# The sixth product of gate ahead of the fifth of value, and the last gate between two scalings

## The chip, the core and the metric

The kernel runs on one core of one Trainium2 chip. The metric is the device time of one execution in microseconds; the runs of the kernel before have a median of 323.09 us (five runs, 322.84 to 324.94). The engines are called as the profile calls them: PE (matrix products; PEld is its weight load), DVE (VectorE), ACT (ScalarE), POOL (GpSimd) and SP, which issues DMAs.

## The reference

Two stages, one after the other. Linear attention without a softmax, with an RMS norm, over 8 batches, 8 heads, 576 tokens and 64 channels a head:

```python
kv = np.einsum('bhsd,bhse->bhde', k, v)
out = np.einsum('bhsd,bhde->bhse', q, kv)
rms = np.sqrt(np.mean(out * out, axis=-1, keepdims=True) + 1e-06)
x = (out / rms * g_norm).transpose(0, 2, 1, 3).reshape(4608, 512)
```

Then a gated feed-forward layer on the 4608 tokens, with 512 channels and 1536 hidden ones:

```python
g, val = x @ w_gate, x @ w_val
ffn_out = gelu(g) * val @ w_out
out = x + sigmoid(x @ w_res) * ffn_out
```

## The kernel before

**Blocks.** The feed-forward layer runs in nine blocks of 512 tokens: block b holds the first 512 tokens of batch b, and block 8 the remaining 64 of all eight. While PE works on block m, the attention of batch m + 2 is done beside it, and its output becomes the input of a later block.

**Seven products.** Most of the layer's products are made by a scheme of seven block products in place of eight: quadrants of tokens and of weights are added beforehand (`ts` are the token sums, `wsg`, `wsv` and `wo_ts` weight sums, `hid_s` sums of the hidden layer), and the partial results are shared through copies and additions.

**A group of gate and value.** `gv_group` (L916) makes four of the twelve slices of the hidden layer, for gate (`g`) and value (`v`) side by side. A string in `ORDERS` (L911) is the order in which every engine is given its work. A word such as `5v` is product 5 of value: four matmuls on PE, each of 128x256. `Eg` and `Ev` are copies on ACT that seed a second PSUM bank with product 1; `dg` and `dv` are copies on ACT that keep product 5; `F` and `c` words are additions on DVE (the sum of bank A and the kept copy); `g11` to `g22` are gelus on ACT; `h11` to `h22` are gelu times value, on DVE except `h22`, which is on POOL. Product 1 opens bank A, 5 opens bank F, 6, 7 and 4 add to bank A, 2 adds to bank E and 3 to bank F. So 6 has to wait until the copy `E` has read bank A, 7 until the addition `F` has read it, and 4 until the addition `c` has. The last group of a block has the order `True`, the others `False`; a dictionary `amid` hangs further work of the attention behind a word.

Blocks 2 to 6 are called whole (`whole`, L1384): all three of their groups are made like this. Block 7 has the groups too, in another sequence.

**The end of a block.** `others` (L709) makes five of the seven products of w_out, each of twelve matmuls, with the gates `pf` (DVE: sigmoid branch times ffn output) between them. The last product, in bank `A`, is followed by the gate of quarter (1, 1) on POOL and the gate of quarter (1, 0) on DVE. `aside(...)` at the names `F`, `00`, `22`, `01`, `11` and `end` is where other work is put in.

**What hangs there.** `plan_attn_ahead` (L1388) puts the norm of batch m + 2 behind `F` and the scalings `a_t` (L334: attention output times inverse norm, one DVE instruction of 128x512 each, four per batch) at the border between blocks. Scalings 0 and 1 go to `11`, ahead of the block's last product (for block 1 the first goes to `01` and the second to `11`); scaling 2 follows the word `1v` of the next block's first group and scaling 3 follows `Fv`, with a DMA transpose behind it. A scaling reads the attention's product from PSUM and so frees its bank.

**Banks.** `banks_of` (L1478) hands the banks on. In the first group of a whole block after another, bank A of gate is the old `D`, A of value the old `E`, E of gate the old `F`, and E of value the old `A`, which the block's last gate, `pf((1, 0), w["A"])`, reads. The banks of `5g` and `5v` are those of the attention's outputs 0 and 1, which scalings 0 and 1 free. So at each border `Ev` waits for the last gate, `5g` for scaling 0 and `5v` for scaling 1.

Each engine takes its instructions in the order in which the program gives them; there is no scheduler behind it.

Of the kernel before, what the change touches and what calls it, by code (L numbers as in the profile page):

```python
# [18 lines left out]
def kernel(  # L19
# [876 lines left out]
    def token_sums(blk, eng):  # L896
# [12 lines left out]
        ]  # L909

    ORDERS = {  # L911
        False: "1g 1v Eg 5g Ev 5v dg 6g dv 6v Fg 2g Fv 2v 7g g11 7v cg 3g cv 3v h11 g12 4g g21 h12 4v g22 h21 h22",
        True: "1g 1v Eg 5g Ev 5v dg 6g dv 6v Fg 2g Fv 2v 7g g11 7v cg 3g cv 3v h11 g22 4g g12 h12 4v g21 h22 h21",
    }

    def gv_group(blk, g, banks, amid, last):  # L916

        if blk not in hids:
            hids[blk] = hidp.tile([P, NF, NJ * P], FP16, tag="hid", name="hid")
        f0 = GF * g  # L920
        ps, ge, sb = {}, {}, {}

        def tile_of(n, u):
            ps[n, u] = pmoe.tile([P, 2, PR], FP32, name=n + u, bank=banks[u, n])
            return ps[n, u]

        def product(p, u):
            ws = wg_c if u == "g" else wv_c
            n = {1: "A", 2: "E", 3: "F", 4: "A", 5: "F", 6: "A", 7: "A"}[p]
            first = p in (1, 5)  # L930
            out_ = tile_of(n, u) if first else ps[n, u]
            s_of = {3: 3, 5: 0, 6: 1, 7: 2}
            t_of = {4: 3, 5: 0, 6: 1, 7: 2}
            quad = {1: (0, 0), 2: (0, 1), 4: (1, 1)}
            xq = {1: (0, 0), 2: (1, 0), 3: (1, 1)}
            for r in range(2):
                for c in range(2):
                    if p in s_of:
                        lhsT = gv_sums[u, g][:, s_of[p], r, c, :]
                    else:  # L940
                        i, k = quad[p]
                        parts = w_quadrant(ws, f0, i, k)
                        lhsT = parts[0][:, r, c, :] if len(parts) == 1 else parts[r][:, 0, c, :]
                    rhs = x_sums[blk][:, t_of[p], :, c, :] if p in t_of else x_quadrant(blk, *xq[p])[:, :, c, :]
                    nc.tensor.matmul(  # L945
                        out_[:, r, :],
                        lhsT=lhsT,
                        rhs=rhs,
                        start=(first and r == 0 and c == 0),
                        stop=(c == 1),  # L950
                        skip_group_check=True,
                    )

        def seed(u):
            nc.scalar.copy(out=tile_of("E", u), in_=ps["A", u])  # L955

        def keep(u):
            sb["d", u] = attnp.tile([P, 2, PR], FP32, tag="sq", bufs=3, name="d")
            nc.scalar.copy(out=sb["d", u], in_=ps["F", u])  # L959

        def plus(u, n):
            if n == "F":
                dst = tile_of("F", u)
            else:
                dst = sb["c", u] = attnp.tile([P, 2, PR], FP32, tag="o32", bufs=3, name="c")
            nc.vector.tensor_tensor(out=dst, in0=ps["A", u], in1=sb["d", u], op=ALU.add)  # L966

        quarter = {"11": ("E", 0, 0), "12": ("F", 0, 1), "21": ("A", 1, 0), "22": ("c", 1, 1)}

        def source(q, u):  # L970
            n = quarter[q][0]
            return sb[n, u] if n == "c" else ps[n, u]

        def gelu(q):
            ge[q] = moep.tile([P, 2, PR], FP16, tag="ge", name="ge")
            nc.scalar.activation(out=ge[q], in_=source(q, "g"), func=AF.Gelu)  # L976

        def hidden(q):
            _, i, j = quarter[q]
            dst = hids[blk][:, f0 + i : f0 + GF : 2, j * PR : (j + 1) * PR]  # L980
            eng = nc.gpsimd if q == "22" else nc.vector
            eng.tensor_tensor(out=dst, in0=ge[q], in1=source(q, "v"), op=ALU.mult)  # L982

        for word in ORDERS[last].split():
            if word[0].isdigit():
                product(int(word[0]), word[1])
            elif word[0] == "E":
                seed(word[1])
            elif word[0] == "d":
                keep(word[1])  # L990
            elif word[0] in "Fc":
                plus(word[1], word[0])
            elif word[0] == "g":
                gelu(word[1:])
            else:
                hidden(word[1:])
            for f in amid.get(word, ()):
                f()
# [120 lines left out]
    first = {}  # L1119
# [219 lines left out]
    amid_out = {}  # L1339
# [15 lines left out]
    def aside_out(blk, ahead_of, *fs):  # L1355
        amid_out.setdefault(blk, {}).setdefault(ahead_of, []).extend(fs)
# [20 lines left out]
    WHOLE = 2  # L1377
    GROUPS = {blk: (1, 2) for blk in range(2, WHOLE)} | {blk: (0, 1, 2) for blk in range(WHOLE, B - 1)} | {B - 1: (1, 0, 2), B: (0, 1, 2)}
    amid_gv = {}
# [4 lines left out]
    def whole(blk):  # L1384

        return WHOLE <= blk < B - 1

    def plan_attn_ahead(b):  # L1388

        rem = pair(b) is not None  # L1390
        m = b - 2
        assert rem == (m in GROUPS)
        act, pool = nc.scalar.copy, nc.gpsimd
        begin = [lambda: attn_begin(b), lambda: d_qT(b)]
        if rem:
            at_word(m, 0, "h22", begin.pop(0), lambda: d_rem_qT(b))
        if m in GROUPS:
            for i in range(2):
                half = lambda i=i: by_token(b, act, slice(2 * i, 2 * i + 2))
                if whole(m):  # L1400
                    at_word(m, i, "g11", half)
                else:
                    at(m, 2 + i, half)
            if whole(m):
                at_word(m, 1, "g11", *begin)
            else:
                at(m, 3, *begin)
            if b + 1 < B:
                at(m, 2 * GF, lambda: load_behind(b))
            last = len(GROUPS[m]) - 1  # L1410
        else:
            at(m, 8, lambda: by_token(b, act, slice(0, 2)))
            at(m, 9, lambda: by_token(b, act, slice(2, 4)), *begin)
            at(m, NF - 1, lambda: a_kv(b, act))
            at(m, NF, lambda: load_behind(b))
        if rem:
            at_word(m + 2, 0, "cv", lambda: a_g(b, NJ, NJ + 1))
            own = 2 * pair(b) + 1 == b
            at_word(m, last, "5v" if own else "3g", lambda: a_rem_kv(b))
            at_word(m, last, "dv" if own else "g12", lambda: kv_out(b))  # L1420
            if own:
                at_word(m, last, "3g", lambda: rem_mm(b))
            at_word(m, last, "g12", lambda: rem_out(b))
        else:
            at(m, NF, lambda: a_o(b), lambda: a_ss(b, 0), lambda: a_ss(b, 1))
            aside_out(m, "D", lambda: a_ss(b, 2), lambda: a_ss(b, 3))
        aside_out(m, "F", lambda: a_norm(b, 0, NJ + rem, pool))
        first = [lambda: new_block(b), lambda: a_t(b, 0), lambda: a_t(b, 1)]
        if m + 1 == WHOLE:
            aside_out(m, "01", *first[0:2])  # L1430
            aside_out(m, "11", first[2])
        elif whole(m + 1):
            aside_out(m, "11", *first)
        else:
            at(m, NF + 3, *first)
        if whole(m + 1):
            t = [lambda j=j: a_t(b, j) for j in range(NJ)]
            if rem:
                at_word(m + 1, 0, "h21", lambda: a_t(b, NJ), lambda: d_xT(b, NJ, NJ + 1))
            for i, word, fs in (  # L1440
                (0, "1v", t[2:3]),
                (0, "Fv", [t[3], lambda: d_xT(b, 0, NJ)]),
                (1, "cv", [lambda: a_g(b, 0, 2)]),
                (2, "Fv", [lambda: a_g(b, 2, NJ)]),
            ):
                at_word(m + 1, i, word, *fs)
            return
        for j in range(2, NJ + rem):
            at(m + 1, j - 2, lambda j=j: a_t(b, j))
        at(m + 1, 1, lambda: d_xT(b, 0, NJ))  # L1450
        at_word(m + 1, 1, "Fv", lambda: a_g(b, 0, 2))
        at_word(m + 1, 1, "cv", lambda: a_g(b, 2, NJ))
# [64 lines left out]
    for blk in range(B + 1):  # L1517
# [21 lines left out]
        else:  # L1539
            slots = [lambda f=f: m_gval(blk, f) for f in range(NF)]  # L1540
            groups = GROUPS.get(blk, ())
            if groups:
# [6 lines left out]
                def group(i, blk=blk, ends=ends):  # L1549
                    if i == 0:  # L1550
                        ends.extend(banks_of(blk))
                        if blk + 2 < B:
                            o = att_at[blk]
                            pattn.opening = o[2:] + o
                    gv_group(blk, GROUPS[blk][i], ends[i], amid_gv.get((blk, i), {}), i == len(GROUPS[blk]) - 1)

                for i in range(len(groups)):
                    slots[n + GF * i] = lambda i=i: group(i)
# [77 lines left out]
```

## Time and profile before

| | |
|---|---|
| median of five runs | 323.09 us (322.84 to 324.94) |
| the profiled execution | 323.7 us, its span 321.9 us |
| mean granted PE clock | 0.996 |
| ACT, idle before `Eg` until PE's bank A | 27.8 us, 8 times |
| DVE, idle before `Fg` until ACT's `d` | 10.0 us, 12 times |
| ACT, idle before `Ev` until PE's bank F | 3.6 us, 5 times |
| DVE scaling `t<-op,ny` | 28 of them, 677 / 682 / 693 ns (lowest, median, highest) |
| DVE gate `osb<-th,wA` | 7 of them, 675 / 677 / 678 ns |
| ACT copy `Ev` | 22 of them, 554 / 570 / 578 ns |

The profile is of one execution. A row of a timeline has the start, the duration, the engine, the line, the operation with its output and inputs, and in brackets how long the engine stood idle before it and which instruction released it. Rows of one engine can overlap, since the next instruction starts before the last has fully ended; the end of a PE row is modelled. Where a wait is for several things, the profile names the one that came last by its own reckoning.

First groups of whole blocks begin at 91.94 us (block 2), 125.20 (3), 158.07 (4), 190.95 (5) and 224.06 (6); block 7 begins at 255.14.

### The profile page before, as it was taken

To read this page: it belongs to the slowest core of one execution; us is meant where nothing else is said; L and a number is where in the kernel's file an instruction comes from. 1 tells how busy PE (TensorE), PEld (TensorE's weight loads), DVE (VectorE), ACT (ScalarE), POOL (GpSimd) and SP (SyncE) were. 2 spreads that over 40 slices of the span, in tenths; PEclk is the share of its full clock that TensorE was granted. 3 is DMA by queue.
4 is the path that set the end of the run, shared out by engine and by line. 5 is a ranking of instruction groups with operands and counts; after the bars stand their busy time and mean duration, and the time that the engine had idled before them with its cause. 6 is when DMAs were issued, how large, how long until landed. Compare 5 with 4: busy or idle time off the path is not lost.

```text
span 321.9 us, 7756 instructions
## 1 busy us (share of the span) xinstructions
PE 312.3 (97%) x3044; PEld 246.9 (77%) x3044; DVE 273.7 (85%) x486; ACT 210.0 (65%) x385; POOL 187.3 (58%) x249
## 2 busy tenths in 40 slices
PE   8999999999999999999999999999999999999993
PEld 3545755444788888888888888888888888888882
DVE  6788879799888899989998999799989677897774
ACT  3773685465838794878487848785767466736770
POOL 2792350573869379757875777516761375396332
PEclk9999999999999999999999999999999999999998
DMA  8999999799994899479947893800340003000204
GB/s 249 327 202 202 195 205 186 168 160 171 170 110 83 196 137 96 81 214 126 105 78 219 107 125 67 227 6 0 68 147 2 0 3 133 0 2 36 97 2 130
DMA packets 76694, 38.90 MB, mean 121 GB/s; under 512 B 42098, under 2 KB 74354, under 8 KB 76658
## 3 DMA queue, kind: packets, MB, share of 16 engines
q0 software_dynamic: 38752, 17.17, 42.1%
q1 hardware_dynamic: 37328, 20.71, 25.2%
q10 hardware_dynamic: 578, 0.52, 0.5%
q8 instruction: 24, 0.39, 0.5%
q14 instruction: 12, 0.10, 0.1%
HBM read 38.80 MB, written 9.44 MB: 150 GB/s over the span
## 4 chain that ended last, share of the span: by engine, by line
PE 83%; DMA 11%; ACT 1%; SPq 1%; DVE 1%; issue 1%; POOL 0%; DVEq 0%; ACTq 0%
PE Av L945 12%; PE wA L515 11%; PE Ag L945 11%; PE Fv L945 6%; PE Fg L945 6%; DMA wo<-in_moe_w_out_dram 5%; PE rA L566 4%; PE gps L410 3%; PE fps L447 3%; PE vps L410 3%; PE wE L515 3%; PE wF L515 3%; PE Ev L945 3%; PE Eg L945 3%; PE wD L515 3%; DMA wg<-in_moe_w_gate_dram 3%
## 5 line engine op out<-in xcount | busy, mean ns | idle before, releaser
L982 POOL TENSOR_TENSOR hid<-ge,c 128x512 f16<-128x512 f16 x22 | 25.6, 1163 | 40.7 <-ACT ge L976 40.7
L515 PEld LDWEIGHTS <-hid_s 128*128 128x128 f16 x384 | 37.6, 98 | 4.5 <-issue 0.2
L945 PEld LDWEIGHTS <-wsv 128*128 128x128 f16 x352 | 33.9, 97 | 7.1 <-issue 2.2
L945 PEld LDWEIGHTS <-wsg 128*128 128x128 f16 x352 | 34.3, 98 | 4.0
L361 POOL TENSOR_TENSOR t<-t,g 128x512 f16<-128x512 f16 x32 | 37.1, 1188 | 0.0
L702 POOL TENSOR_TENSOR osb<-osb,t 128x512 f32<-128x512 f32 x28 | 34.1, 1247 | 0.0
L955 ACT COPY Eg<-Ag 128x512 f32<-128x512 f32 x22 | 12.8, 582 | 27.8 <-PE Ag L945 27.8
L515 PEld LDWEIGHTS <-hid 128*128 128x128 f16 x288 | 28.2, 98 | 3.5
L945 PEld LDWEIGHTS <-wg 128*128 128x128 f16 x264 | 25.8, 98 | 3.2
L945 PEld LDWEIGHTS <-wv 128*128 128x128 f16 x264 | 25.8, 98 | 3.2
L966 DVE TENSOR_TENSOR Fg<-Ag,d 128x512 f32<-128x512 f32 x22 | 15.3, 697 | 14.8 <-ACT d L959 10.0
L945 PE MATMUL Av<-ts,wsv 128*128 128x256 f16 x176 | 26.4, 272 | 1.2 <-ACT Ev L955 1.1
L945 PE MATMUL Ag<-ts,wsg 128*128 128x256 f16 x176 | 26.4, 273 | 0.0
L258 DVE TENSOR_REDUCE ss<-sq 128x8 f32<-128x512 f32 x32 | 20.5, 679 | 2.4 <-ACT sq L253 2.4
L398 ACT ACTIVATE ge<-gps 128x512 f16<-128x512 f32 x20 | 11.7, 597 | 14.3 <-PE gps L410 14.1
L515 PE MATMUL wA<-wo_ts,hid_s 128*128 128x256 f16 x168 | 20.6, 272 | 0.0
L976 ACT ACTIVATE ge<-Eg 128x512 f16<-128x512 f32 x22 | 13.1, 597 | 9.7 <-PE Eg L945 9.7
L976 ACT ACTIVATE ge<-c 128x512 f16<-128x512 f32 x22 | 13.7, 625 | 7.8 <-DVE c L966 7.8
L345 DVE TENSOR_TENSOR t<-op,ny 128x512 f16<-128x512 f32 x28 | 18.4, 683 | 0.5 <-POOL ny L319 0.4
L976 ACT ACTIVATE ge<-Fg 128x512 f16<-128x512 f32 x22 | 13.0, 591 | 8.8 <-PE Fg L945 6.5
L966 DVE TENSOR_TENSOR c<-Ag,d 128x512 f32<-128x512 f32 x22 | 15.1, 688 | 4.2 <-PE Ag L945 4.2
L410 PE MATMUL gps<-xT,wg 128*128 128x512 f16 x72 | 18.5, 379 | 0.0
(219 smaller groups left out, 857.8 us busy)
## 6 DMA issues: line engine op xcount, KB each, us to landing
out_dram<-osb SPq DMA_DIRECT2D x14, 512.0 KB, 3.6
qraw<-in_q_dram POOLq DMA_DIRECT2D x7, 512.0 KB, 6.6
k<-in_k_dram POOLq DMA_DIRECT2D x7, 512.0 KB, 8.5
v<-in_v_dram POOLq DMA_DIRECT2D x7, 512.0 KB, 10.6
wg<-in_moe_w_gate_dram POOLq DMA_DIRECT2D x2, 512.0 KB, 8.4
wv<-in_moe_w_val_dram POOLq DMA_DIRECT2D x2, 512.0 KB, 9.0
wo<-in_moe_w_out_dram POOLq DMA_DIRECT2D x2, 512.0 KB, 14.5
out_dram<-osb SPq DMA_DIRECT2D x4, 256.0 KB, 4.5
```

What stands on the lines that cost most here:

```text
L258: nc.vector.tensor_reduce(out=out_, in_=sqs.pop((b, i)), op=ALU.add, axis=mybir.AxisListType.X)
L345: nc.vector.tensor_tensor(out=t, in0=o, in1=scale, op=ALU.mult)
L361: eng.tensor_tensor(out=t_t[blk][:, jj, :], in0=t_t[blk][:, jj, :], in1=g16, op=ALU.mult)
L410: nc.tensor.matmul(ps[:, j0 * P : j1 * P], lhsT=w[:, cc, :], rhs=xT_t[blk][:, j0:j1, cc, :], start=(cc == 0 and j0 == 0), stop=(cc == NP - ...
L515: nc.tensor.matmul(ps[:, e - es[0], :], lhsT=a[:, f, e * P : (e + 1) * P], rhs=b[:, f, :], start=(start and e == es[0] and f == 0), stop=( ...
L566: nc.tensor.matmul(out_[:, e, :], lhsT=x_[:, e, cc, :], rhs=w_[:, cc, :], start=(first and e == 0 and cc == 0), stop=(cc == 1), skip_group ...
L702: nc.gpsimd.tensor_tensor(out=res_all[of], in0=res_all[of], in1=t_t[blk][of], op=ALU.add)
L945: nc.tensor.matmul(out_[:, r, :], lhsT=lhsT, rhs=rhs, start=(first and r == 0 and c == 0), stop=(c == 1), skip_group_check=True,)
L955: nc.scalar.copy(out=tile_of("E", u), in_=ps["A", u])
L966: nc.vector.tensor_tensor(out=dst, in0=ps["A", u], in1=sb["d", u], op=ALU.add)
L976: nc.scalar.activation(out=ge[q], in_=source(q, "g"), func=AF.Gelu)
L982: eng.tensor_tensor(out=dst, in0=ge[q], in1=source(q, "v"), op=ALU.mult)
```

## The change

A third order, `None`, is used for the first group of the whole blocks 2 to 6. It reads `5g 6g Ev 5v dg 6v dv` where `False` reads `5g Ev 5v dg 6g dv 6v`. On PE this puts the four matmuls of `6g` ahead of those of `5v`; ACT's order stays `Eg`, `Ev`, `dg`, `dv`.

At the border ahead of these blocks, scaling 1 moves from `11` (ahead of the last product and the last gate) to the front of `end` (behind the last gate). On DVE the order becomes scaling 0, gate (1, 0), scaling 1, scaling 2 in place of scaling 0, scaling 1, gate, scaling 2. In block 1 two token sums stood at `end`, and scaling 1 goes ahead of them.

```diff
     ORDERS = {
+        None: "1g 1v Eg 5g 6g Ev 5v dg 6v dv Fg 2g Fv 2v 7g g11 7v cg 3g cv 3v h11 g12 4g g21 h12 4v g22 h21 h22",
         False: "1g 1v Eg 5g Ev 5v dg 6g dv 6v Fg 2g Fv 2v 7g g11 7v cg 3g cv 3v h11 g12 4g g21 h12 4v g22 h21 h22",
...
-    def gv_group(blk, g, banks, amid, last):
+    def gv_group(blk, g, banks, amid, order):
...
-        for word in ORDERS[last].split():
+        for word in ORDERS[order].split():
...
         first = [lambda: new_block(b), lambda: a_t(b, 0), lambda: a_t(b, 1)]
-        if m + 1 == WHOLE:
-            aside_out(m, "01", *first[0:2])
-            aside_out(m, "11", first[2])
-        elif whole(m + 1):
-            aside_out(m, "11", *first)
+        if whole(m + 1):
+            aside_out(m, "01" if m + 1 == WHOLE else "11", *first[0:2])
+            amid_out[m].setdefault("end", []).insert(0, first[2])
...
-                    gv_group(blk, GROUPS[blk][i], ends[i], amid_gv.get((blk, i), {}), i == len(GROUPS[blk]) - 1)
+                    order = None if i == 0 and whole(blk) else i == len(GROUPS[blk]) - 1
+                    gv_group(blk, GROUPS[blk][i], ends[i], amid_gv.get((blk, i), {}), order)
```

## The prediction

> **What bounds the kernel now.** I read the page's busy line first, then PE's rows in the list of waits, then the timelines of PE, VectorE (DVE) and ScalarE (ACT) around the start of a block.
>
> ```profile
> PE 312.3 (97%) x3044; PEld 246.9 (77%) x3044; DVE 273.7 (85%) x486; ACT 210.0 (65%) x385; POOL 187.3 (58%) x249
> ```
>
> PE is the bound: 9.6 us of the span are left beside its busy time, more than half of them in the first and last of the page's forty slices. So the change can only win what PE stands still for. The list of PE's waits has one row after 60 us:
>
> ```profile
> PE Av L945 <- ACT Ev L955: 1.1, 5, 0.2
> ```
>
> The timeline puts the five at 107.17 (third group of block 2, outside the change) and at 127.78, 160.66, 193.53 and 226.63: the sixth product of value ("6v") in the first group of blocks 3 to 6. Block 3 on PE, a row per product of four matmuls:
>
> ```profile
> 125.20 0.60 PE L945 MATMUL Ag<-xT,wg 128*128 128x256 f16 x4
> 125.64 0.60 PE L945 MATMUL Av<-xT,wv 128*128 128x256 f16 x4
> 126.07 0.60 PE L945 MATMUL Fg<-ts,wsg 128*128 128x256 f16 x4
> 126.53 0.60 PE L945 MATMUL Fv<-ts,wsv 128*128 128x256 f16 x4
> 126.97 0.60 PE L945 MATMUL Ag<-ts,wsg 128*128 128x256 f16 x4
> 127.78 0.60 PE L945 MATMUL Av<-ts,wsv 128*128 128x256 f16 x4 [0.22 <-ACT Ev L955]
> ...
> 129.09 0.60 PE L945 MATMUL Ag<-ts,wsg 128*128 128x256 f16 x4
> 129.62 0.60 PE L945 MATMUL Av<-ts,wsv 128*128 128x256 f16 x4
> ...
> 131.40 0.60 PE L945 MATMUL Av<-ts,wv 128*128 128x256 f16 x4
> ```
>
> These are 1g, 1v, 5g, 5v, 6g, 6v, then 7g, 7v and 4v, the last of the group's fourteen. Undisturbed products start 0.437 us apart (the second group of block 2: 13 steps in 99.31 to 104.99). So the cost is larger than the 0.22 shown, since a row ends 0.16 after the next can start: 6v is 0.37 late, 7v 0.09, 5v 0.02, 4v 0.03. From 1g to 4v that is 131.40 - 125.20 - 13 x 0.437 = 0.52 us per block. Now the two engines that feed it:
>
> ```profile
> 124.55 0.67 DVE L698 TENSOR_TENSOR osb<-th,wF 128x512 f32<-128x512 f32 x1
> 125.19 1.29 DVE L345 TENSOR_TENSOR t<-op,ny 128x512 f16<-128x512 f32 x2
> 126.40 0.68 DVE L698 TENSOR_TENSOR osb<-th,wA 128x512 f32<-128x512 f32 x1
> 126.99 0.68 DVE L345 TENSOR_TENSOR t<-op,ny 128x512 f16<-128x512 f32 x1
> 128.27 0.70 DVE L966 TENSOR_TENSOR Fg<-Ag,d 128x512 f32<-128x512 f32 x1 [0.59 <-ACT d L959]
> 128.88 0.69 DVE L966 TENSOR_TENSOR Fv<-Av,d 128x512 f32<-128x512 f32 x1
> ```
>
> ```profile
> 125.84 0.57 ACT L955 COPY Eg<-Ag 128x512 f32<-128x512 f32 x1 [3.54 <-PE Ag L945]
> 127.16 0.57 ACT L955 COPY Ev<-Av 128x512 f32<-128x512 f32 x1 [0.75 <-PE Fv L945]
> 127.64 0.59 ACT L959 COPY d<-Fg 128x512 f32<-128x512 f32 x1
> 128.12 0.60 ACT L959 COPY d<-Fv 128x512 f32<-128x512 f32 x1
> ```
>
> The copy Ev goes into the bank that the last gate (osb<-th,wA) reads; the gate ends at 127.08 and Ev starts at 127.16. The profile names PE's Fv (5v) as releaser, because that ends at 126.53 + 0.60 = 127.13. Block 2 tells the two apart:
>
> ```profile
> 93.76 0.57 ACT L955 COPY Ev<-Av 128x512 f32<-128x512 f32 x1 [0.62 <-DVE osb L698]
> ```
>
> Its gate ends at 93.68, while its 5v, started at 93.25, ends only at 93.85: Ev starts before 5v is over, so it waits for the gate. Latencies read from these rows: DVE to PE 0.05, DVE to ACT 0.08, ACT to PE 0.05, PE to ACT 0.04, ACT to DVE 0.04; a DVE row starts 0.60 after the one before.
>
> **The change, part by part.** No instruction is added or removed; in the built program only PE and DVE change order, and ACT, POOL and SP issue the same lists, so no DMA moves in its queue (the transpose behind the fourth scaling comes with it, 0.46 earlier).
>
> *The gate goes ahead of the second scaling* (blocks 2 to 6). In block 3 the first scaling keeps 125.19, the gate takes 125.79 to 126.47, the second scaling 126.40 to 127.08, and the third stays at 126.99. The gate also waits for the last product of w_out (ends 125.36); queued behind it would be the scalings, but it is ready 0.4 us ahead of its new place, so this wait costs nothing. Ev can start at 126.55 instead of 127.16 and ends at 127.12.
>
> *5v waits for the second scaling*, which frees its bank: from 127.08 + 0.05 = 127.13 on, 0.6 later than now. Left in its place (126.51) it would stall 0.62.
>
> *6g goes ahead of 5v* and fills that hole. It waits for the copy Eg (ends 126.41, so 126.46) and PE reaches it at 126.51: no stall; it could slip to 126.69 before it pushed 5v. PE is free for 5v at 126.95; 5v starts at 127.13: **a new stall of 0.18**. Then 6v at 127.57 (Ev done at 127.17), against 127.78.
>
> *Downstream.* d(Fg) runs 127.03 to 127.62, so Fg starts at 127.66 (0.61 earlier). d(Fv) waits for 5v (127.73) and runs 127.77 to 128.37; Fv 128.41 to 129.10 (0.47 earlier). 7g is due at 128.88 and Fg ended at 128.35; 7v is due at 129.32, Fv allows 129.15: the 0.09 stall goes. 4g is due at 130.63 and its sum c ends at 130.29; 4v at 131.06, with its c ended at 130.89. So 4v starts at 131.06 against 131.40: **0.34 us per block**. What is late next is DVE in the second group: there Fv ends at 135.66 and 7v starts at 135.76, hardly any room. But DVE runs without a pause from Fv of the first group up to there and is itself 0.46 earlier, more than PE's 0.34.
>
> Blocks 4, 5 and 6 have the same rows (4v at 164.27, 197.15, 230.25 against 163.94, 196.80, 229.91 by the same steps): 0.33, 0.35, 0.34.
>
> *Block 2 gives nothing.* There DVE has two token sums behind the gate and no pause from 91.80 on, and both orders hold the same instructions:
>
> ```profile
> 94.87 0.70 DVE L966 TENSOR_TENSOR Fg<-Ag,d 128x512 f32<-128x512 f32 x1
> ```
>
> Fg has no idle before it. 6v moves from 94.39 to 94.17, but Fv still starts at 95.48 and holds 7v at 96.22.
>
> *One rule against the row.* The Trainium skill, "VectorE: DVE Perf Modes", section "The DRAIN you can't avoid", says that after a VectorE operation the next starts only once the pipeline has emptied (and allows that some start earlier). Taken strictly, with 0.68 a step from the end of osb<-th,wF at 125.22, the second scaling would end at 127.26, 5v start at 127.31, and a block win 0.16: 0.6 in all. The rows start 0.60 apart while lasting 0.68, here and in each of the blocks, so I take 0.60.
>
> *Buffers.* In the built program one gelu of block 2's second group now waits for POOL, and one of its third no longer; block 3 has it the other way round. The gelu starts at 104.81, and the POOL row it needs ended at 100.52: nothing either way.
>
> Sum: 0 + 0.34 + 0.33 + 0.35 + 0.34 = **1.36 us**. Behind the stage PE is without other waits to the end but the one at 107.17, which lies ahead. The profiled execution took 323.7 us (span 321.9): it would take 322.3. It stands 0.6 above the median of the runs shown, 323.09, so against that I forecast **321.7 us**, 0.42% faster.
>
> **The rivals.**
> - *Hidden anyway.* DVE proves to be the limit in blocks 3 to 6 too, as it is in block 2, and hands the time back in the second group: 0 to 0.6 won (the strict rule above is inside), about 322.9. For it: DVE at 85%, the 0.05 to 0.1 of room before 7v. Against: 0.59 idle before each Fg.
> - *More than reckoned.* 5v isn't held by the second scaling and all gaps close: 4 x 0.52 plus block 2's 98.01 - 91.94 - 13 x 0.437 = 0.39, together 2.5: 320.6. Partly so, without 5v's 0.18: 2.1, 321.0. Against: DVE has no pause that would bring the scaling forward.
> - *Slower.* Ev does wait for 5v, as the profile's row says. Then 5v at 127.13 puts Ev at 127.77 to 128.34, 6v at 128.39 and, by way of d and Fv, 7v at 130.23: 0.61 later than now, in each of five blocks 3.0: 326.1. It decides as soon as Ev starts later than 127.16. Against it stands block 2's row, where Ev started with 5v still running.
>
> **How the numbers follow.** A difference of 0.5%, 1.6 us, is about what a measurement of this kernel can tell from no change. The forecast has 0.70, hidden 0.12, more 0.13, slower 0.05. The forecast's own spread (321.2 to 322.3: steps read to 0.02 us twenty times over, and medians that move by 0.3) has about a quarter beyond 321.5, so faster gets 0.16 + 0.13 = 0.29, slower 0.05, and 0.66 stays within. The range runs from 320.7, near all gaps closed, to 323.2, nothing won.
>
> **What would show it.** In the new trace: in blocks 3 to 6 the stall sits at 5v with about 0.18 between starts beyond 0.437, DVE named as its cause, and none at 6v; Ev starts 0.6 earlier relative to 1g; Fg's idle before it is gone or tiny; 1g to 4v takes 5.86 instead of 6.20, while block 2 keeps 6.07. I am wrong if 6g stalls on Eg, if 7v is still late in blocks 3 to 6, or if PE waits anew in the second group.

## The result, and the profile after

The changed kernel has a median of 321.94 us (321.27 to 329.68, 31 runs; the highest is a disturbed execution and is left out of the ratio) against 323.04 us before (52 runs): ratio 0.9955, interval 0.9945 to 0.9966. By the ratio 1.45 us (1.10 to 1.78) are won, 1.10 by the medians; 1.36 were forecast.

Its profiled execution has a span of 320.2 us, 1.7 shorter than the one before. Of that, 0.38 us lies ahead of block 2 (its first product starts at 91.56 against 91.94), where the change has not begun; that is scatter between executions (the one before waited 0.62 us for a DMA at 43.34, the one after did not). From there to the first product of block 7 it is 161.81 us against 163.20: 1.39 us.

PE in the first group of block 3, the same rows as before (start, duration, engine, line, operation):

```profile
124.79 0.60 PE L946 MATMUL Ag<-xT,wg 128*128 128x256 f16 x4
125.23 0.60 PE L946 MATMUL Av<-xT,wv 128*128 128x256 f16 x4
125.66 0.60 PE L946 MATMUL Fg<-ts,wsg 128*128 128x256 f16 x4
126.10 0.60 PE L946 MATMUL Ag<-ts,wsg 128*128 128x256 f16 x4
126.72 0.60 PE L946 MATMUL Fv<-ts,wsv 128*128 128x256 f16 x4
127.15 0.60 PE L946 MATMUL Av<-ts,wsv 128*128 128x256 f16 x4
...
128.46 0.60 PE L946 MATMUL Ag<-ts,wsg 128*128 128x256 f16 x4
128.90 0.60 PE L946 MATMUL Av<-ts,wsv 128*128 128x256 f16 x4
...
130.65 0.60 PE L946 MATMUL Av<-ts,wv 128*128 128x256 f16 x4
```

6g now follows 5g, and the one step that isn't 0.44 is the one into 5v: 126.72 - 126.10 = 0.62, so 5v is 0.18 late. 6v and 7v follow without a gap. From 1g to 4v it is 130.65 - 124.79 = 5.86 us, against 6.20.

DVE and ACT in the same stretch:

```profile
124.14 0.67 DVE L698 TENSOR_TENSOR osb<-th,wF 128x512 f32<-128x512 f32 x1
124.78 0.69 DVE L345 TENSOR_TENSOR t<-op,ny 128x512 f16<-128x512 f32 x1
125.39 0.68 DVE L698 TENSOR_TENSOR osb<-th,wA 128x512 f32<-128x512 f32 x1
125.98 1.28 DVE L345 TENSOR_TENSOR t<-op,ny 128x512 f16<-128x512 f32 x2
127.26 0.70 DVE L967 TENSOR_TENSOR Fg<-Ag,d 128x512 f32<-128x512 f32 x1
127.97 0.70 DVE L967 TENSOR_TENSOR Fv<-Av,d 128x512 f32<-128x512 f32 x1
```

```profile
125.43 0.57 ACT L956 COPY Eg<-Ag 128x512 f32<-128x512 f32 x1 [3.54 <-PE Ag L946]
126.16 0.57 ACT L956 COPY Ev<-Av 128x512 f32<-128x512 f32 x1 [0.16 <-DVE osb L698]
126.64 0.59 ACT L960 COPY d<-Fg 128x512 f32<-128x512 f32 x1
127.35 0.59 ACT L960 COPY d<-Fv 128x512 f32<-128x512 f32 x1
```

The gate is now the second row behind the bank F gate, and Ev's releaser is named as that gate; the idle of 0.59 us ahead of Fg is gone.

The first group of each whole block, from the start of 1g to that of 4v (us):

| block | before | after | forecast |
|---|---|---|---|
| 2 | 6.07 | 6.05 | 6.07 |
| 3 | 6.20 | 5.86 | 5.86 |
| 4 | 6.20 | 5.86 | 5.87 |
| 5 | 6.20 | 5.86 | 5.85 |
| 6 | 6.19 | 5.85 | 5.85 |

### The profile page after: what moved, and what is told of

Its sections match the earlier page's. It is cut to its first block, busy times and chain, and to the rows that moved or that the text cites. A ratio compares the mean times of both kernels' runs of the same rounds, so it can differ in the third digit from the quotient of the medians.

```text
span 320.2 us, 7756 instructions
## 1 busy us (share of the span) xinstructions
PE 311.7 (97%) x3044; PEld 247.2 (77%) x3044; DVE 274.9 (86%) x486; ACT 210.6 (66%) x385; POOL 187.2 (58%) x249
## 4 chain that ended last, share of the span: by engine, by line
PE 95%; DVE 3%; issue 0%; ACT 0%; DVEq 0%
PE Av L946 12%; PE Ag L946 12%; PE wA L515 12%; PE Fv L946 6%; PE Fg L946 6%; PE gps L410 5%; PE vps L410 5%; PE rA L566 4%; PE fps L447 3%; PE Eg L946 3%; PE Ev L946 3%; PE wD L515 3%; PE wF L515 3%; PE wE L515 3%; PE w L515 2%; PE idle L1111 2%
```

## The experiments

All ratios are to the kernel before, run beside it on the same chip, with the 95% interval.

### The two halves of the change alone

`gate_only`: the changed kernel with the old order of products.

```diff
-                    order = None if i == 0 and whole(blk) else i == len(GROUPS[blk]) - 1
+                    order = i == len(GROUPS[blk]) - 1
```

> The gate ahead of scaling 1 in blocks 2 to 6, but the old order of products. My theory (5v waits for scaling 1, wherever it stands): in blocks 3 to 6 5v starts 0.6 us late right behind 5g, 6g and 6v follow without a wait, 1g to 4v takes 6.30 us against 6.20 before and 5.86 in the changed kernel; block 2 takes 6.16. Some 0.5 us slower than before, ratio 1.0015. Rival (the gate's place alone brings the gain, the order of products is idle decoration): 1.4 us faster, ratio 0.9957, 5.86 us in these blocks.

Measured: 0.9999 (0.9981 to 1.0017). 1g to 4v takes 6.28 us in blocks 3, 4 and 5, 6.27 in block 6 and 6.14 in block 2: the mechanism is as expected, to 0.02 us. PE in block 3:

```profile
125.05 0.60 PE L946 MATMUL Fg<-ts,wsg 128*128 128x256 f16 x4
126.09 0.60 PE L946 MATMUL Fv<-ts,wsv 128*128 128x256 f16 x4 [0.44 <-DVE t L345]
```

5v waits for the scaling (`t`), here 0.60 us, and the profile names it. The 0.39 us that the five groups lose don't show in the time: in the trace block 2's third group, outside the change, became 0.5 us shorter. The last part of the experiments shows how.

`order_only`: the changed kernel with scaling 1 back ahead of the gate.

```diff
-        if whole(m + 1):
-            aside_out(m, "01" if m + 1 == WHOLE else "11", *first[0:2])
-            amid_out[m].setdefault("end", []).insert(0, first[2])
+        if m + 1 == WHOLE:
+            aside_out(m, "01", *first[0:2])
+            aside_out(m, "11", first[2])
+        elif whole(m + 1):
+            aside_out(m, "11", *first)
```

> The new order of products in blocks 2 to 6, but scaling 1 still ahead of the gate. My theory (6v waits for Ev, and Ev for the gate): 5v follows 6g without a stall, 6v still starts 0.37 us late behind Ev, 1g to 4v stays at 6.20 us in blocks 3 to 6 and 6.07 in block 2; ratio to before 1.000. Rival (Ev waits for 5v, as the profile's row of before names it): with 5v 0.44 us later Ev, 6v and 7v are some 0.4 us later, 6.6 us a block, 2 us slower, ratio 1.006. Rival (the order alone brings the gain): ratio 0.9957.

Measured: 1.0001 (0.9983 to 1.0019); 6.19 us in blocks 3 to 6, 6.05 in block 2. The rows of PE and ACT that decide it:

```profile
127.48 0.60 PE L946 MATMUL Fv<-ts,wsv 128*128 128x256 f16 x4
128.30 0.60 PE L946 MATMUL Av<-ts,wsv 128*128 128x256 f16 x4 [0.22 <-ACT Ev L956]
```

```profile
127.68 0.57 ACT L956 COPY Ev<-Av 128x512 f32<-128x512 f32 x1 [0.74 <-PE Ag L946]
```

Ev starts at 127.68, 0.40 us before 5v (`Fv`) ends. So it does not wait for 5v, and the slower rival falls. The profile now names 6g (`Ag`) as the releaser, because that ended last before it (127.64); the gate had ended at 127.59. In the changed kernel Ev starts at 126.16, with 6g, started at 126.10, still running: it does not wait for 6g either. Neither half brings anything by itself: with the gate alone 5v waits in place of 6v, with the order alone 6v waits as before.

### Block 2

`not_block2`: both edits for blocks 3 to 6 alone (the new order of products only where `blk > WHOLE`, and the old place of scaling 1 ahead of block 2).

> The change in blocks 3 to 6 alone, block 2 as before. My theory (block 2 gains nothing because VectorE has no pause there): block 2 keeps 6.07 us from 1g to 4v, blocks 3 to 6 have 5.86; the time equals that of the changed kernel, ratio to before 0.9957. Rival (each of five borders carries a fifth): 0.28 us is lost, ratio 0.9966.

Measured: 0.9954 (0.9937 to 0.9971); block 2 has 6.06 us, blocks 3 to 6 have 5.84 to 5.85. The interval holds the rival's 0.9966 too; the trace is what shows that the border of block 2 carries next to nothing.

`sums_ahead`: the changed kernel with the special case of block 2's token sums taken out.

```diff
-        if blk == 2:
-            aside_out(blk - 1, "00", *t[0:2])
-            aside_out(blk - 1, "end", *t[2:4])
-            continue
```

> The changed kernel with block 2's last two token sums placed as in blocks 3 to 6: one ahead of the sum of bank A, one ahead of scaling 0, where VectorE idles 0.78 and 0.39 us. My theory (the two sums behind scaling 1 are what holds block 2): Fg starts about 0.6 and Fv 0.4 us earlier there, 1g to 4v in block 2 falls from 6.05 to about 5.72 us, blocks 3 to 6 stay at 5.86; some 0.3 us faster than the changed kernel, ratio to before 0.9947. Rival (GpSimd's rows, freed 2 us earlier by this, slow VectorE, or d is what holds Fg): block 2 stays at 6.0 us or gets longer, ratio 0.9957 or above.

Measured: 0.9929 (0.9909 to 0.995), block 2's first group 5.81 us in place of 6.05: 0.24 won of the 0.33 expected; blocks 3 to 6 have 5.83 to 5.85. Scaling 0 still waited for the norm there and came 0.07 us later than reckoned, so the copy Eg, 6g and 5v were 0.03 to 0.10 late. So the two sums were what held block 2. But border to border block 2 became 0.75 us shorter, not 0.24. That led to the last section.

### What holds the last 0.17 us

Three kernels on top of `sums_ahead` ask what sets scaling 1 in blocks 3 to 6, where 5v is still 0.17 us late: VectorE's queue, or the norm on GpSimd, whose last row ends 0.03 us before scaling 0 starts.

`sum3_behind` takes one row from VectorE's queue ahead of scaling 0:

```diff
-        for key, f in zip(("00", "00", "22", "01") if whole(blk) else ("00", "22", "01", "11"), t):
+        for key, f in zip(("00", "00", "22", "end" if blk > 2 else "01") if whole(blk) else ("00", "22", "01", "11"), t):
```

> As sums_ahead, and in blocks 3 to 6 the fourth token sum moves from ahead of the gate of bank F to behind scaling 1, so that VectorE has 0.33 us less to do ahead of scaling 0. My theory: scaling 0 also waits for the norm, whose last row on GpSimd ends 0.03 us before it, so scaling 0, the gate and scaling 1 stay where they are, 5v keeps its 0.17 us, and Fg comes 0.3 us or more later: 1g to 4v 5.85 to 6.1 us in these blocks, no faster than sums_ahead, ratio to before 0.993 to 0.995. Rival (VectorE's queue alone sets scaling 1): 5v's stall goes, 5.68 us, ratio 0.9910.

Measured: 0.9957 (0.9929 to 0.9985), 6.01 to 6.03 us. The group's time is in the expected range and the ratio just above it (0.993 to 0.995), but I had only half of the reason: 5v was on time. The norm came 0.19 us earlier as well, since its next to last row took 0.31 us instead of 0.49 when the token sum no longer ran beside it. The loss came behind scaling 1, where the moved sum took 0.78 us in place of 0.41 beside a row of GpSimd: 7g was 0.14 and 7v 0.16 us late, and 4v 0.04.

`norm_short` is `sums_ahead` with two instructions of the norm (L317 and L318) left out.

> As sums_ahead, but the norm on GpSimd leaves out the last two instructions of its second refinement (a multiplication and an addition, some 0.9 us), so its values differ. My theory: the norm ends 0.9 us earlier, but VectorE has no pause ahead of scaling 0, so 5v keeps its 0.17 us and 1g to 4v stays at 5.85 us in blocks 3 to 6; in block 2, where VectorE does pause ahead of scaling 0, the 0.13 us there go. Ratio 0.993. Rival (the norm alone holds scaling 0): 5.68 us, ratio 0.991.

Measured: 1.0095 (1.0061 to 1.013), slower by 5 us than `sums_ahead`: 6.89 us in blocks 3 to 6, and 6.42 in block 2. Both theories fell. DVE and POOL in block 3:

```profile
123.28 1.51 DVE L475 TENSOR_TENSOR ts<-xT,ts 128x512 f16<-128x512 f16 x1
124.71 0.68 DVE L695 TENSOR_TENSOR osb<-th,wF 128x512 f32<-128x512 f32 x1
125.31 0.68 DVE L342 TENSOR_TENSOR t<-op,ny 128x512 f16<-128x512 f32 x1
```

```profile
123.01 0.27 POOL L316 TENSOR_TENSOR ny<-nh,ny 128x40 f32<-128x40 f32 x1
123.24 1.27 POOL L695 TENSOR_TENSOR osb<-th,osb 128x512 f32<-128x512 f32 x1
```

The norm is done earlier, so GpSimd's gate starts earlier, at 123.24, and the token sum, which starts 0.04 us later, takes 1.51 us instead of 0.41. That pushed scaling 0 back, and the next 5g was 0.89 us late.

`both_short` has both edits.

> Both edits together: the fourth token sum behind scaling 1, and the norm without its last two instructions, so its values differ. My theory: scaling 0 starts 0.33 us earlier relative to 1g, the gate follows when the last product has ended, scaling 1 ends in time, and 5v no longer stalls in blocks 3 to 6. What of the 0.17 us remains by 4v depends on the sum behind scaling 1, which delays Fg: 5.68 to 5.85 us, ratio 0.991 to 0.993. Rival (something else holds 5v): its 0.17 us stay.

Measured: 1.003 (1.0007 to 1.0052). 5v's stall is gone in blocks 3 to 6, but the moved sum took 1.26 us there and 7g was 0.5 us late: 6.38 to 6.39 us. What remains of the 0.17 us is thus not free: VectorE's row can be moved, but not to where GpSimd is busy.

`norm_short_hold` tests the collision: as `norm_short`, but GpSimd's gate first waits for the token sum.

```diff
+                nc.gpsimd.tensor_copy(out=hold, in_=x_sums[blk + 1][0:1, 3, 1, 1, 0:1])
                 pf((1, 1), c22, nc.gpsimd)
```

> As norm_short (the norm leaves out two instructions, so its values differ), with a tiny copy on GpSimd ahead of its gate that waits for the fourth token sum, so that the gate, whose operands are all in SBUF, no longer runs beside that sum. In norm_short that sum took 1.51 us against 0.41 and scaling 0 came 0.9 us late. My theory (the two rows hinder each other when they run together): the sum is back at 0.41 to 0.5 us, 5g is on time, 5v is 0.17 us late or less, 1g to 4v at 5.85 us or less in blocks 3 to 6, ratio to before 0.993 instead of 1.0095. Rival (the sum is long for another reason, the norm's changed values or a wait inside it): it keeps 1.5 us and the ratio stays at 1.009.

Measured: 0.9928 (0.9908 to 0.9948), 5.79 to 5.80 us in blocks 3 to 6 and 5.68, no gap at all, in block 2. The same two engines:

```profile
124.36 0.41 DVE L475 TENSOR_TENSOR ts<-xT,ts 128x512 f16<-128x512 f16 x1
```

```profile
124.84 0.18 POOL L730 COPY hold<-ts 1x1 f16<-1x1 f16 x1 [0.47 <-DVE ts L475]
124.97 1.26 POOL L695 TENSOR_TENSOR osb<-th,osb 128x512 f32<-128x512 f32 x1
```

With one more wait on GpSimd the sum and the gate no longer run together, the sum takes 0.41 us again, and the kernel is 1.7% faster than without the wait: the collision is shown.

### Filling the hole further

`hole_sums`: on top of `sums_ahead`, 2g is moved ahead of 5v as well, 3g ahead of 7v, and scaling 3 behind the sum `c` of value.

```diff
-        None: "1g 1v Eg 5g 6g Ev 5v dg 6v dv Fg 2g Fv 2v 7g g11 7v cg 3g cv 3v h11 g12 4g g21 h12 4v g22 h21 h22",
+        None: "1g 1v Eg 5g 6g Ev 2g 5v dg 6v dv Fg 2v Fv 7g g11 3g 7v cg cv 3v h11 g12 4g g21 h12 4v g22 h21 h22",
...
-                (0, "Fv", [t[3], lambda: d_xT(b, 0, NJ)]),
+                (0, "cv", [t[3], lambda: d_xT(b, 0, NJ)]),
```

> As sums_ahead, with the second product of gate ahead of 5v as well, the third of gate ahead of the seventh of value, and scaling 3 behind the sum c of value. My theory (VectorE is next, as it has hardly a pause up to the second group): 5v's stall goes and 1g to 4v falls to about 5.74 us in blocks 3 to 6, but VectorE now waits for later products of value, its rows of the second group's start come 0.3 us or more later, and PE pays it back there: border to border no faster than sums_ahead, up to 0.4 us a block slower, ratio 0.993 to 0.998. Rival (the 0.17 us are free to take): 0.5 us faster, ratio 0.9915.

Measured: 1.0033 (1.0005 to 1.0062). In the first group of blocks 3 to 6 all is as expected: 5.74 to 5.75 us, 5v on time. In the second group of block 4 PE then stands still, longer than expected:

```profile
168.94 0.60 PE L946 MATMUL Ev<-xT,wv 128*128 128x256 f16 x4
170.17 0.60 PE L946 MATMUL Ag<-ts,wsg 128*128 128x256 f16 x4 [0.63 <-DVE Fg L967]
```

```profile
167.88 1.63 DVE L345 TENSOR_TENSOR t<-o,ny 128x512 f16<-128x512 f32 x1
169.43 0.68 DVE L967 TENSOR_TENSOR Fg<-Ag,d 128x512 f32<-128x512 f32 x1
```

7g is 0.79 us late behind Fg, and Fg stands behind a fifth scaling (of the tokens for block 8, both operands in SBUF), which took 1.63 us here, 1.32 in `sums_ahead` and 1.14 in the kernel before. So VectorE is the next limit there, and on top of its later start it met GpSimd's rows at a worse moment. Up to 0.4 us a block was expected; from border to border blocks 4 to 6 became 0.94 to 0.95 us longer than in `sums_ahead`, block 2 0.45 longer, and block 3 0.10 shorter. How much of the loss in blocks 4 to 6 is the later start and how much the meeting was not separated.

### The version that beats both, once more

> The changed kernel once more, to compare on one chip with sums_again: ratio to before 0.9955, block 2 6.05 us from 1g to 4v and its third group's 6v 0.36 us late.

> The same kernel as sums_ahead, beside the changed kernel on one chip. My theory: border to border block 2 is 0.75 us shorter than in the changed kernel (0.24 in its first group, 0.5 in its third, where the multiplication by g took 0.48 us instead of 1.48), ratio to before 0.993. Rival (the 0.75 us were one execution's luck): block 2 as in the changed kernel, ratio 0.9955.

Measured on one chip: the changed kernel 322.00 us, ratio 0.9961 (0.9939 to 0.9982); with the token sums moved 321.20 us, ratio 0.9938 (0.9915 to 0.9961). The medians are 0.8 us apart, though the intervals overlap. From the first product of block 2 to that of block 7 the traces have 161.74 and 161.03 us: the 0.7 us is no accident of one execution (the first ones of the two kernels had 161.81 and 161.01). The spans of the two profiled executions, 320.2 and 320.4, don't show it, because in that of `sums_again` PE waited 1.24 us for a DMA at 80.83. `sums_ahead` waited there too, 1.33 us; `sum3_behind`, which has the same instructions up to there, did not. The 0.7 us comes from two places: 0.22 us in the first group (6.03 and 5.81), and the rest in the third. There the changed kernel had

```profile
103.38 1.49 DVE L370 TENSOR_SCALAR xT<-xT,gcol 128x1024 f16<-128x1024 f16 x1
103.43 1.16 POOL L702 TENSOR_TENSOR osb<-osb,t 128x512 f32<-128x512 f32 x1
```

and `sums_again`

```profile
104.05 0.48 DVE L370 TENSOR_SCALAR xT<-xT,gcol 128x1024 f16<-128x1024 f16 x1
104.13 1.41 POOL L702 TENSOR_TENSOR osb<-osb,t 128x512 f32<-128x512 f32 x1
```

In both the multiplication by g ran beside GpSimd's four additions of the residual; the POOL row is the fourth of them. With 1.49 us, the hidden layer's rows behind it come late, and 6v of the third group is 0.36 us late; in the kernel before that was the wait at 107.17. With 0.48 us it isn't late at all; the cost is GpSimd's, whose four rows take 4.75 us instead of 4.50. `gate_only` had 0.48 and 1.41 as well, which is where its half microsecond came from.

## Why the prediction was right

- **PE bound, and the four stalls at 6v are what can be won.** Right. No other stage changed by more than the scatter.
- **Ev waits for the gate.** Right: relative to 1g it starts at 1.37 us after the change (forecast 1.35, before 1.96), and `order_only` excludes a wait for 5v.
- **5v then waits for scaling 1, and 6g fills the hole, with 0.18 us left over.** Right to 0.01 us: 5v starts 1.93 us behind 1g, as forecast. `gate_only` shows what 6g in the hole is worth: 6.28 against 5.86 us.
- **Downstream.** Fg at 2.47 us behind 1g (forecast 2.46), Fv at 3.18 (3.21), 7v at 4.11 (4.12), 4v at 5.86 (5.86); nothing is paid back in the second group, but that was close (see below).
- **Block 2 gives nothing.** Right, 0.02 us, and for the reason given: with the two token sums ahead of the gate, its first group won 0.24 us.
- **0.60 us a step on DVE.** Right; the strict form of the rule would have left 0.6 us of the gain. The scaling behind the gate starts at 125.98, 0.59 behind it, and 5v comes 0.18 and not 0.36 us late.
- **What was off.** The sum is 1.36 us against 1.39 in the trace. I expected the profile to name DVE at 5v. It names nothing: 6g, started at 126.10, is drawn to its modelled end at 126.70, so that of the 0.18 us only 0.02 look idle, and only the start times show the loss.
- **Where luck came in: the second group.** The forecast had VectorE 0.46 us earlier up to there, more than PE's 0.34, because its rows follow each other without a pause. They do, but one of them, a fifth scaling (of the tokens for block 8, both operands in SBUF), grew from 1.40 to 1.59 us in block 3. In the kernel before:

```profile
133.06 1.40 DVE L345 TENSOR_TENSOR t<-o,ny 128x512 f16<-128x512 f32 x1
134.98 0.68 DVE L966 TENSOR_TENSOR Fv<-Av,d 128x512 f32<-128x512 f32 x1
```

and in the changed one, with PE's 7v:

```profile
132.16 1.59 DVE L345 TENSOR_TENSOR t<-o,ny 128x512 f16<-128x512 f32 x1
134.28 0.68 DVE L967 TENSOR_TENSOR Fv<-Av,d 128x512 f32<-128x512 f32 x1
135.01 0.60 PE L946 MATMUL Av<-ts,wsv 128*128 128x256 f16 x4
```

Relative to 1g, Fv started at 9.78 us before and at 9.49 after: 0.29 earlier, less than PE's 0.34. Fv ends at 134.96, and 0.05 later 7v starts. The 0.05 us of room that the forecast saw ahead of this 7v is used up to the last hundredth, in block 4 too (1.14 to 1.33 us, Fv 0.30 earlier). That 7v isn't late was luck and not the reason given.
- **Where luck came in: the third group of block 2.** The forecast left its wait of 0.37 us alone as outside the change. `gate_only` made it go, with a shift of a few hundredths; the changed kernel did not.

## What to carry to other kernels

When a wait on the bound engine is due to the order in another engine's queue, write down the start times of all three queues with the measured step and latency of each: moving the awaited instruction up makes another one late, and the gain is only there if the bound engine has work for just that hole. Measure the loss by the distances between starts, not by the idle time shown. And after moving work in time, look at the rows of VectorE and GpSimd whose operands are all in SBUF: two that meet can cost more than the move brings.

## What the runs showed that was not expected

VectorE rows with all their operands in SBUF were prolonged by up to about one GpSimd row when they met it: a token sum 1.51 us against 0.41 (`norm_short`, GpSimd's row 1.27), the multiplication by g 1.49 against 0.48 (GpSimd's rows 1.15 each), while scalings and gates that read PSUM stayed at 0.67 to 0.69 us beside the same rows. The Trainium skill, "SBUF — State Buffer", section "Who interferes with whom", states that a VectorE instruction contends with GpSimd when it has two SBUF inputs (and GpSimd reads SBUF) or runs in a mode that uses two ports, and that whoever issues first gets the shared pair of ports for the whole instruction while the other blocks. These numbers agree with it in size. `norm_short_hold`, which made GpSimd's gate wait until the sum had ended, brought the sum back to 0.41 us.

Which of the two is held up hung on hundredths of a microsecond. In all thirteen traces here the multiplication by g in block 2 starts just ahead of GpSimd's fourth addition. In six of them (before, after, `order_only`, `not_block2`, `hole_sums`, `after_again`) it starts 0.01 to 0.05 us ahead, and it takes 1.45 to 1.49 us and the addition 1.15 to 1.16. In the other seven it starts 0.07 to 0.10 us ahead, and it takes 0.48 us and the addition 1.40 to 1.42. So one of the two always runs undisturbed, as the page has it, but a row that starts first in the profile can still be the one that has to wait. No run moved this start alone.
